# First two batches of a fused attention and mixing kernel: a scaled Abs in the weight conversion, softmax sums on VectorE, second-batch keys from transposed sums, and a searched order

## The chip, the cores and the metric

The kernel runs on one core of one Trainium2 chip. The metric is the device time of one execution in microseconds, taken as the median of three runs. A profiled execution of the same program gives the trace from which all rows below are taken.

## The reference, cut to what matters

Eight batches of 576 tokens go through three layers. The first is attention over 8 heads of 64 columns, with keys and values averaged over groups of 8 tokens (72 groups). The second turns the result by an angle and mixes tokens with two 576 by 576 matrices; the third is another pair of mixers, which the change does not touch.

```python
k_p = k.reshape(B, H, Sp, pool, D).mean(axis=3)          # pool = 8, Sp = 72
scores = scale * np.matmul(q, k_p.transpose(0, 1, 3, 2))
attn = np.exp(scores - np.max(scores, axis=-1, keepdims=True))
attn = attn / (np.sum(attn, axis=-1, keepdims=True) + 1e-09)
x = np.matmul(attn, v_p)                                  # then (B, 576, 512)
...
theta = x @ w_theta
yr = np.einsum('ts,bsd->btd', w_tok_r, x * np.cos(theta))
yi = np.einsum('ts,bsd->btd', w_tok_i, x * np.sin(theta))
u = x + yr + yi
u = u + np.maximum(u @ w_ch, 0.0)
```

The weights arrive as 64-bit floats and are converted to 32 bits on the chip.

## The kernel before, in words

The function `first_batches` holds batch 0 and the first part of batch 1, together with the conversion of `w_theta` and the nine 128-row slices of the two token mixers. It does not issue instructions directly. It hands each piece of work to a `Plan` as an operation with its engine, its estimated length and what it depends on; `Plan.run` then walks through time with a list scheduler and issues the operations in the order it finds. Later batches are written out by hand-set due times. At the very end a second scheduler, `Arrange`, takes the whole recorded program and fixes each engine's final order. So a change to the estimates or to the work of `first_batches` moves instructions on all engines.

The steps of batch 0, with the names that appear in the rows:

- **Keys.** `k` is loaded transposed (head columns on partitions), VectorE sums groups of 8 tokens into `sums`, and small copies put the scaled sums into `bdk`. For batch 1 the kernel before loads `k` with tokens on partitions (`nat_k`) instead, and TensorE sums the groups with a small matrix `pool`: per head pair four matmuls of 16 columns and two of 8 (line 420, `x<-pool,nat_k`).
- **Softmax.** TensorE forms scores (`x<-bdk,q`), VectorE takes the extreme per row (`mx`), ScalarE evaluates exponentials in 20 instructions of 72 columns per head pair, of which each also accumulates its sum (`e,ss<-x,mx`, line 2100). VectorE or GpSimd then scales `e` by the reciprocal `sm`.
- **Attend and angle.** `e` is transposed (`tp`, line 434), multiplied with the pooled values (`pt,vb`), giving `R`; five groups of four-pass 32-bit matmuls with `wt`, the converted `w_theta`, give the angle; sines follow, and `Z` (with a high and a low part) is x times cosine and sine.
- **Conversion.** 26 pieces: 8 of `w_theta`, 256 columns wide, and 18 of the token mixers, 288 columns wide. ScalarE takes the absolute value of the upper word, VectorE raises it to a floor (`most`, line 1951), shifts it by three bits and masks (line 1962), puts in the sign (line 1967) and the low bits (line 1972). For a mixer piece ScalarE then writes a rounded high part (`wtk`, line 1992) and GpSimd the remainder (line 1995).
- **Mixing.** 8 groups of 27 matmuls per batch, `m<-wtk,Z`. The first four take the first half of `Z`; groups of 256 columns need the first nine mixer pieces, groups of 320 columns need all 18. Each group goes through high times high, then the low part of `wtk`, then the low part of `Z`.

TensorE is kept busy while it has nothing else by `keep_busy`: matmuls of 512 columns on a constant tile (line 430, `m<-busy`), whose number the plan sets from its own estimate of the gap.

Of the kernel before, what the change touches and what calls it, by code (L numbers as in the profile page):

```python
# [57 lines left out]
F64_FLOOR = 2.0 ** -15  # L58
TH = ((0, 256), (256, 320))
TG = (2, 0, 1)  # L60
GUARD = range(26)
NK = 4
WARM = 800.0
LOWS = ()
WS = (0, 1)
ZL = (1, 1, 1)
EDVE = (2, 3)
NEAR = 20.0
# [3 lines left out]
class Arrange:  # L72
# [43 lines left out]
    def price(self, i):  # L116
# [27 lines left out]
        if e == "Activation":  # L144
            f = str(getattr(self.ins[i], "func", ""))
            table = "exp" if "Exp" in f else "sin" if "Sin" in f else None
            if op == "TensorCopy":
                return n * 0.833 + (52.0 if ps else 100.0), False, None
            return n * 0.833 + (62.0 if ps else 112.0) + (75.0 if len(ins) > 1 else 0.0), False, table
# [176 lines left out]
def tile_attn_moe(  # L326
# [1364 lines left out]
    class Plan:  # L1691

        LAT = {"PE": 170.0, "DVE": 110.0, "ACT": 120.0, "POOL": 110.0, "SP": 0.0}

        def __init__(self):
            self.ops = []
            self.users = {}
            self.dma = 3400.0  # L1700

        def add(self, ways, deps=(), homes=(), take=None, give=()):
            if isinstance(ways, tuple):
                ways = [ways]
            o = dict(ways=ways, deps=list(deps), take=take, give=give)
            for h in homes:
                o["deps"] += h.prior
                h.users.append(o)
            self.ops.append(o)
# [5 lines left out]
        def run(self, idle):  # L1715
            table = None
            for o in self.ops:
                o["rank"] = 0.0
            for o in reversed(self.ops):
                e, ns = o["ways"][0][0:2]  # L1720
                o["rank"] += (ns if e != "SP" else 2000.0) + self.LAT[e]
                for d in o["deps"]:
                    d["rank"] = max(d["rank"], o["rank"])
            free = {e: 0.0 for e in self.LAT}
            lock = 0.0
            todo = list(self.ops)
            while todo:
                best = []
                sp = False
                for o in todo:  # L1730
                    if any("end" not in d for d in o["deps"]):
                        continue
                    ready = max([0.0] + [d["end"] for d in o["deps"]])
                    if o["take"] is not None:
                        if not o["take"].free:
                            continue
                        ready = max(ready, o["take"].free[0][0])
                    for w in o["ways"]:
                        if w[0] == "SP":
                            if sp:  # L1740
                                continue
                            sp = True
                        s = max(ready, free[w[0]], lock + (90.0 if w[0] == "POOL" else 0.0) if w[2] is True else 0.0)
                        d = w[1]
                        if w[2] in ("exp", "sin") and w[2] != table:
                            d += 1290.0
                        best.append((s, s + d, o, w))
                s0 = min(b[0] for b in best)
                near = [b for b in best if b[0] <= s0 + NEAR]
                top = max(b[2]["rank"] for b in near)  # L1750
                o = [b[2] for b in near if b[2]["rank"] == top][0]
                s, end, o, w = min((b for b in best if b[2] is o), key=lambda b: b[1])
                todo.remove(o)
                e = w[0]
                if e == "PE":
                    idle(s, s - free["PE"])
                free[e] = end
                if w[2] is True:
                    lock = end
                elif w[2] is not False and e == "ACT":  # L1760
                    table = w[2]
                o["end"] = end + self.LAT[e]
                if e == "SP" and w[2]:
                    self.dma = max(self.dma, s + 3000.0) + w[2] * 1000.0 / 370.0
                    o["end"] = self.dma
                if o["take"] is not None:
                    o["take"].last = o["take"].free.pop(0)[1]
                w[3]()
                for g in o["give"]:
                    g.done(o["end"])  # L1770
# [15 lines left out]
    class Slots:  # L1786
        def __init__(self, names):
            self.free = [(0.0, n) for n in names]
            self.last = None

    class Held:


        def __init__(self, pool, readers):
            self.pool, self.n, self.t = pool, readers, 0.0
# [4 lines left out]

        def done(self, t):
            self.n -= 1
            self.t = max(self.t, t)
            if self.n == 0:
                self.pool.free.append((self.t, self.tag))
                self.pool.free.sort()

    def first_batches():
# [16 lines left out]
        EXP = 200.0  # L1825
# [4 lines left out]
        def ac(n):  # L1830
            return n * 0.86 + 65.0

        def po(n):
            return n * 2.1 + 147.0
# [25 lines left out]
        kn = {}  # L1860
# [31 lines left out]
        def fetch_k_pair(b, p):  # L1892
            h = kn[b]
            ds = slice(p * 128, (p + 1) * 128)
            k_at[b, p] = fetch(lambda: h()[:, 0:4, ds],
                               k01[b, 0:512, ds].rearrange("(c p) d -> p c d", p=128), 256, [h])

# [16 lines left out]
        kt_at = {}  # L1914
        for p in range(4):
            if p < NK:
                fetch_k_summed(0, p)
            elif p == NK:
                kn[0] = home("R0", [128, 5, 512], F32, "nat_k0")
                kt_at = {0: fetch_tail(kn[0], k01[0])}  # L1920
            if p >= NK:
                fetch_k_pair(0, p)
# [10 lines left out]
        def add_piece(i):  # L1933
# [10 lines left out]
            def absf():  # L1944
# [8 lines left out]
            def relu():  # L1953
                nc.scalar.activation(out=m_(), in_=m_(), func=ACTF.Relu, bias=floor[:, 0:1])

            def back():
                nc.gpsimd.tensor_scalar(
                    out=m_(), in0=m_(), scalar1=1.0, scalar2=F64_FLOOR, op0=ALU.mult, op1=ALU.add)

            def shl():  # L1960
                mu = m_().bitcast(U32)
                nc.vector.tensor_scalar(out=mu, in0=mu, scalar1=3, scalar2=0x3FFFFFFF,
                                        op0=ALU.logical_shift_left, op1=ALU.bitwise_and)

            def sign():
                mu = m_().bitcast(U32)
                nc.vector.scalar_tensor_tensor(out=mu, in0=box["t"][:, :, 1], scalar=0xC0000000, in1=mu,
# [7 lines left out]
            o = add(("ACT", ac(n), False, absf), [at], hs, take=mids)  # L1975
            if i in GUARD:
                o = add(("DVE", n * 0.521 + 65, True, most), [o], hs)
            else:
                o = add(("ACT", ac(n) + 60, False, relu), [o], hs)
                o = add(("POOL", n * 1.0 + 90, True, back), [o], hs)  # L1980
# [3 lines left out]
            if kind == "th":  # L1984
                conv[what[:3]] = add(("ACT", ac(n), False, lambda: nc.scalar.activation(
# [11 lines left out]
            x = add(("ACT", ac(n), False, hi), [o], hs + [w], give=[hold])  # L1997
# [13 lines left out]
        left = {}  # L2011

# [734 lines left out]
```

## Time and profile before

| | |
|---|---|
| median of three runs | 1255.43 us (1254.73 to 1256.89) |
| the profiled execution | 1259.36 us, span 1257.6 us |
| mean granted TensorE clock | 0.991 |
| TensorE busy | 1243.9 us (99%) |
| VectorE busy | 958.0 us (76%) |
| ScalarE busy | 672.1 us (53%) |
| GpSimd busy | 298.9 us (24%) |

The span runs from the first to the last instruction. Busy time of TensorE counts a matmul at a lowered clock, or one on the constant tile, like any other, so 99% does not say that all of it was needed work.

### The profile page before, as it was taken

How to read it: one execution, taken by the hardware profiler on the slowest of the kernel's cores; microseconds unless marked ns; L12 is line 12 of the kernel's file. 1: busy time of each engine (PE TensorE's matmuls, PEld its weight loads, DVE VectorE, ACT ScalarE, POOL GpSimd, SP SyncE). 2: the span in 40 equal slices, each digit the busy share in tenths (PEclk: the TensorE clock that was granted, in tenths of full speed). 3: DMA queues.
4: the chain of work that ended last, by engine and by line, in shares of the span. 5: the costliest groups of instructions: out<-in, count | busy, mean ns of one | idle time of the engine just before them, and what ended most of it. 6: DMA issues, size and time to landing. Idle time of an engine off the chain costs nothing.

```text
span 1257.6 us, 22368 instructions
## 1 busy us (share of the span) xinstructions
PE 1243.9 (99%) x8121; PEld 1207.9 (96%) x8123; DVE 958.0 (76%) x1723; ACT 672.1 (53%) x1405; POOL 298.9 (24%) x306
## 2 busy tenths in 40 slices
PE   8999999999999999999999999999999999999998
PEld 5889999999999999999999999999999999999998
DVE  6978868586767797867875679888644598988894
ACT  7887566666657564334322256666554544443442
POOL 1254423233241532211110011221000032123212
PEclk9979999999999999999999999999999999999999
DMA  9524323232321123657782487977448966546621
GB/s 339 162 70 136 126 93 97 68 114 70 109 71 54 38 84 125 233 195 250 251 296 76 158 273 250 299 250 249 160 138 306 342 225 220 173 141 220 207 84 69
DMA packets 122127, 214.51 MB, mean 171 GB/s; under 512 B 11744, under 2 KB 68576, under 8 KB 122016
## 3 DMA queue, kind: packets, MB, share of 16 engines
q1 hardware_dynamic: 122016, 213.08, 50.9%
q8 instruction: 64, 1.05, 0.3%
q14 instruction: 47, 0.39, 0.1%
HBM read 134.39 MB, written 78.64 MB: 169 GB/s over the span
## 4 chain that ended last, share of the span: by engine, by line
PE 92%; DVE 3%; DMA 2%; ACT 2%; issue 1%; POOL 0%; SPq 0%; DVEq 0%; ACTq 0%; POOLq 0%
PE m L420 33%; PE x L420 31%; PE t L420 23%; PE x L434 3%; ACT e L2100 1%; DMA scr_x<-u 1%; DMA ws<-w_ch 1%; DMA raw_e<-scr_g 0%; PE m L430 0%; PE t L434 0%; DVE raw_n L1416 0%; DVE u L1211 0%; PE m L434 0%; DMA scr_g<-p 0%; DVE ope_Xh L1413 0%
## 5 line engine op out<-in xcount | busy, mean ns | idle before, releaser
L420 PE MATMUL m<-wtk,Z 128*128 128x256 f32 (+1 forms) x1536 | 255.9, 302 | 1.3 <-ACT wtk L1992 1.3
L420 PEld LDWEIGHTS m<-wtk,Z 128*128 128x128 f32 x1536 | 222.7, 191 | 4.2 <-ACT wtk L1992 3.0
L420 PE MATMUL x<-ope_Z,wa 128*128 128x384 f32 x492 | 94.8, 336 | 0.0
L420 PEld LDWEIGHTS x<-ope_Z,wa 128*128 128x128 f32 x492 | 86.4, 188 | 0.0
L1665 POOL TENSOR_TENSOR o<-o,u 128x384 f32<-128x384 f32 x12 | 16.4, 1386 | 268.4 <-DMA raw_Z<-scr_g 167.1
L1034 POOL TENSOR_TENSOR Z<-tmp,Z 128x1024 fp32r<-128x1024 f32 x26 | 63.2, 2442 | 69.5 <-ACT Z L1033 69.5
L1314 POOL TENSOR_TENSOR wo<-wm,wo 128x256 fp32r<-128x256 f32 (+2 forms) x36 | 31.1, 867 | 180.3 <-ACT wo L1313 174.0
L420 PE MATMUL t<-wth,Xh 128*128 128x256 f32 x448 | 62.2, 279 | 0.0
L420 PE MATMUL m<-wtk,zt 128*128 128x256 f32 (+1 forms) x192 | 57.8, 302 | 0.3 <-ACT wtk L1992 0.3
L420 PEld LDWEIGHTS t<-wth,Xh 128*128 128x128 f32 x448 | 57.5, 188 | 0.5
L420 PE MATMUL m<-ope_Z,wa 128*128 128x384 f32 x234 | 48.2, 336 | 0.0
L420 PE MATMUL t<-ope_Z,wa 128*128 128x384 f32 x234 | 48.0, 335 | 0.0
L1019 DVE TENSOR_TENSOR tmp<-x,tmp 128x1024 f32<-128x1024 f32 x26 | 31.7, 1220 | 18.0 <-PE x L434 15.3
L420 PE MATMUL x<-ope_R,wa 128*128 128x384 f32 x228 | 43.8, 337 | 0.0
L420 PE MATMUL x<-bdk,q 128*128 128x144 f32 x298 | 43.2, 296 | 0.4 <-ACT bdk L2014 0.4
L420 PE MATMUL t<-ope_Xl,wa 128*128 128x384 f32 x204 | 42.4, 336 | 0.0
L420 PE MATMUL m<-ope_Xl,wa 128*128 128x384 f32 x204 | 42.3, 336 | 0.0
L420 PEld LDWEIGHTS x<-bdk,q 128*128 128x128 f32 x298 | 40.3, 198 | 1.5 <-ACT bdk L2014 1.1
L420 PEld LDWEIGHTS m<-ope_Z,wa 128*128 128x128 f32 x234 | 41.5, 188 | 0.0
L420 PEld LDWEIGHTS t<-ope_Z,wa 128*128 128x128 f32 x234 | 41.4, 188 | 0.0
L1299 POOL TENSOR_TENSOR wsum<-wm 128x128 f32<-128x128 f32 (+1 forms) x18 | 12.4, 690 | 119.4 <-DVE wm L1289 118.6
L1574 DVE TENSOR_TENSOR p<-p,u 128x384 f32<-128x384 f32 x36 | 20.5, 568 | 26.5 <-ACT p L1573 26.5
(480 smaller groups left out, 3544.0 us busy)
## 6 DMA issues: line engine op xcount, KB each, us to landing
wa<-scr_w SPq DMA_DIRECT2D x42, 512.0 KB, 5.4
scr_g<-g SPq DMA_DIRECT2D x108, 192.0 KB, 3.0
scr_w<-wo SPq DMA_DIRECT2D x42, 256.0 KB, 3.4
scr_u<-R SPq DMA_DIRECT2D x32, 288.0 KB, 2.1
u<-scr_u SPq DMA_DIRECT2D x32, 288.0 KB, 4.2
scr_w<-wo SPq DMA_DIRECT2D x18, 512.0 KB, 5.7
scr_x<-u SPq DMA_DIRECT2D x32, 288.0 KB, 2.2
raw_n<-scr_x SPq DMA_DIRECT2D x24, 384.0 KB, 4.1
```

Of the source, the lines that this page charges most:

```text
L420: nc.tensor.matmul(out=o, lhsT=l, rhs=r, start=start, stop=stop, skip_group_check=skip)
L434: nc.tensor.transpose(o, i, ident)
L1019: nc.vector.tensor_tensor(out=tmp, in0=px.unsqueeze(1).to_broadcast([128, 2, 512]), in1=tmp, op=ALU.mult)
L1034: later(1.0 if lo is nc.vector else 0.0, lambda: lo.tensor_sub(out=zl, in0=zv, in1=zh.bitcast(F32)), tg, zg)
L1299: nc.gpsimd.tensor_tensor(out=s[:, 2], in0=a11, in1=a21, op=ALU.subtract)
L1314: eng.tensor_sub(out=o[:, :, 1], in0=src, in1=o[:, :, 0].bitcast(F32))
L1574: nc.vector.tensor_add(out=p5[ih].t, in0=p5[ih].t, in1=u2[ih].t)
L1665: nc.gpsimd.tensor_tensor(out=u22[d].t, in0=u22[d].t, in1=u2[d].t, op=ALU.add)
L2100: nc.scalar.activation(out=e()[:, c, 2 * p + h, :], in_=box["v"][:, c - c0, h], func=ACTF.Exp, scale=-1.0, bias=mx[i][:, c, h:h + 1], accu ...
```

## The change

Six things are edited, all within the first two batches:

1. The absolute value in the conversion carries a scale of 2 to the -112, and the floor instruction `most` goes (26 of them). The shift loses its mask, and the sign mask changes from two bits to one.
2. The 80 exponentials of the first two batches no longer accumulate; per head pair one VectorE reduction over 720 columns forms the sums.
3. The keys of batch 1 are loaded transposed and summed on VectorE, as batch 2 already did; the 24 matmuls with `pool` and their copies go.
4. Nine of the 18 low parts of `wtk`, and the four low parts of the split `w_theta`, move from GpSimd to VectorE.
5. The plan's estimates of latencies and lengths change, and a search of 400 seeded variations of the priorities picks the order with the lowest estimated end.
6. `Arrange` counts 92 ns more for a ScalarE instruction with two outputs.

The core of the diff:

```diff
+TRIES = 400
+SEED = 2
+LOWS = range(0, 26, 2)
+WS = (1, 2)
+SOFTMAX = "BBBBBBBB"
...
-                nc.scalar.activation(out=m_(), in_=box["t"][:, :, 1].bitcast(F32), func=ACTF.Abs)
-
-            def most():
-                nc.vector.tensor_scalar(out=m_(), in0=m_(), scalar1=F64_FLOOR, scalar2=None, op0=ALU.max)
+                nc.scalar.activation(out=m_(), in_=box["t"][:, :, 1].bitcast(F32), func=ACTF.Abs, scale=F64_SCALE)
...
-                nc.vector.tensor_scalar(out=mu, in0=mu, scalar1=3, scalar2=0x3FFFFFFF,
-                                        op0=ALU.logical_shift_left, op1=ALU.bitwise_and)
+                nc.vector.tensor_scalar(out=mu, in0=mu, scalar1=3, scalar2=None, op0=ALU.logical_shift_left)
...
         def keys(b, p):
-            if (b, p) in ks_h:
+            if b == 0:
                 return keys_summed(b, p)
...
-                for c in range(4):
-                    mm(o[:, 8 + 16 * c:24 + 16 * c], kh()[:, c, ds], pm()[:, 0:16], True, True)
-                for c0 in (0, 72):
-                    mm(o[:, c0:c0 + 8], kh()[0:64, 4, ds], pm()[0:64, 0:8], True, True)
...
+            if p % 2 == 0:
+                pair_at[b] = next_keys(b, p // 2)
+            return pair_at[b]
...
-                                bias=mx[i][:, c, h:h + 1], accum_out=ss[i][:, c, h:h + 1])
+                                bias=mx[i][:, c, h:h + 1], **acc)
...
+            if mode != "C":
+                es = [add(("DVE", dv(720), False, lambda: nc.vector.tensor_reduce(
+                    out=ss[i], in_=ep(), axis=AX.X, op=ALU.add)), es + last.get(("ss", i), []), [e])]
...
+            for _ in range(tries):
+                p = list(prio)
+                k = draw.randrange(n)
+                v = draw.choice((-30e3, -10e3, -4e3, -1.5e3, 1.5e3, 4e3, 10e3, 30e3))
+                for i in range(k, min(n, k + draw.choice((1, 1, 2, 4, 8, 16)))):
+                    p[i] += v
+                c, o = self.trial(p)
+                if c <= cost:
+                    prio, cost, out = p, c, o
```

The order moves in three places that matter below. First TensorE, at the end of the angle's matmuls of batch 0 (`wt,R`; `con,R` are transposes of the result). Before, the last of them are followed by the key sums of batch 1 and the first mixing matmuls:

```order
L434 MATMUL t_651<-con,R_423 128x128 x4
L434 MATMUL x_658<-con,R_423 128x128 x4
L420 MATMUL t_666<-pool,nat_k_386 128x16 x4
L420 MATMUL t_666<-pool,nat_k_386 128x8 x2
L420 MATMUL m_782<-wtk_502,Z_584 128x256
L420 MATMUL m_782<-wtk_505,Z_584 128x256
```

In the changed program the same place reads:

```order
L423 MATMUL x_569<-wt_386,R_407 128x256 x8
L423 MATMUL x_602<-wt_386,R_407 128x256
L423 MATMUL m_592<-wtk_538,Z_558 128x256
L423 MATMUL m_592<-wtk_481,Z_558 128x256
L423 MATMUL m_592<-wtk_483,Z_558 128x256
L423 MATMUL m_592<-wtk_567,Z_558 128x256
```

The matmuls with `pool` are gone, and the first mixing group (`m_592`) starts inside the last angle group.

Second VectorE, at the end of the softmax of batch 0. Before:

```order
L2114 TENSOR_SCALAR sm_106<-ss_104 128x10
L2117 RECIPROCAL sm_106<-sm_106 128x10
L2121 TENSOR_TENSOR e<-e,sm_106 128x5x144
L1844 COPY pt_341<-x_326 128x320
L2114 TENSOR_SCALAR sm_107<-ss_105 128x10
L2117 RECIPROCAL sm_107<-sm_107 128x10
L2121 TENSOR_TENSOR e<-e,sm_107 128x5x144
```

Changed, two sums over 720 columns stand ahead of the two scalings:

```order
L2170 TENSOR_REDUCE ss_104<-e 128x5x2
L2172 TENSOR_SCALAR sm_106<-ss_104 128x10
L2175 RECIPROCAL sm_106<-sm_106 128x10
L2170 TENSOR_REDUCE ss_105<-e 128x5x2
L2179 TENSOR_TENSOR e<-e,sm_106 128x5x144
L2172 TENSOR_SCALAR sm_107<-ss_105 128x10
L2175 RECIPROCAL sm_107<-sm_107 128x10
L2179 TENSOR_TENSOR e<-e,sm_107 128x5x144
```

Third TensorE again, where in the changed program the first group of 320 columns (`m_760`) begins. It is the first that needs the second halves of `wtk`, and it comes right behind the pooled values of batch 1:

```order
L423 MATMUL x_734<-nat_v_645,pool 128x512 x4
L423 MATMUL m_760<-wtk_538,Z_558 128x320
L423 MATMUL m_760<-wtk_481,Z_558 128x320
L423 MATMUL m_760<-wtk_483,Z_558 128x320
L423 MATMUL m_760<-wtk_567,Z_558 128x320
L423 MATMUL m_760<-wtk_560,Z_558 128x320
L423 MATMUL m_760<-wtk_496,Z_558 128x320
L423 MATMUL t_773<-bdk,q_271 128x144 x3
L423 MATMUL m_760<-wtk_625,Z_558 128x320
L423 MATMUL m_760<-wtk_578,Z_558 128x320
L423 MATMUL m_760<-wtk_447,zt_616 128x320
```

Before, the first such group is likewise behind the two groups of 256 columns, but batch 1's scores stand ahead of it there, and here only one part of them does (`t_773`).

## Rows read from the trace of the kernel before

**Rows 1.** The page: busy time by engine, and the granted clock in 40 slices.

```profile
PE 1243.9 (99%) x8121; PEld 1207.9 (96%) x8123; DVE 958.0 (76%) x1723; ACT 672.1 (53%) x1405; POOL 298.9 (24%) x306
...
PEclk9979999999999999999999999999999999999999
```

**Rows 2.** Windows: stretch, length, busy per engine, granted clock, DMA share and rate.

```profile
22.00:50.00 28.00, 27.67 (x123) 20.57 (x123) 27.08 (x74) 24.36 (x60) 5.59 (x7) 1.00 0.85 270
58.28:71.94 13.66, 13.66 (x61) 13.54 (x60) 7.33 (x25) 9.16 (x45) 0.06 (x1) 0.50 0.15 44
85.59:92.42 6.83, 6.53 (x24) 5.85 (x24) 5.44 (x15) 6.80 (x32) 6.42 (x9) 0.50 0.23 73
55.00:110.00 55.00, 52.69 (x301) 47.54 (x302) 44.47 (x97) 44.93 (x162) 30.74 (x29) 0.81 0.29 90
```

**Rows 3.** Timeline of TensorE up to 54 us: start, length, instructions, idle before.

```profile
9.91 1.03 PE L430 MATMUL m<-busy 128*128 128x512 bf16 x4
...
12.02 2.75 PE L430 MATMUL m<-busy 128*128 128x512 bf16 x11
...
25.50 0.77 PE L420 MATMUL x<-pt,vb 128*128 128x320 f32 x2
26.60 0.78 PE L420 MATMUL x<-t,vl 128*128 128x320 f32 x2 [0.33 <-DVE vl L2190]
...
30.02 0.60 PE L434 MATMUL x<-con,e 128*128 128x128 f32 x4
...
34.34 7.07 PE L420 MATMUL x<-wt,R 128*128 128x256 f32 x32
...
53.77 1.50 PE L420 MATMUL t<-pool,nat_k 128*128 128x16 f32 x12
```

**Rows 4.** Windows of the instructions on `nat_k` alone: their four stretches summed.

```profile
sum 8.18, PE 8.17 PEld 7.95; mean PE 2.04 PEld 1.99
```

**Rows 5.** Timeline of ScalarE: the first exponentials and the last.

```profile
8.61 0.32 ACT L2100 ACTIVATE e<-x,mx 128x72 f32<-128x72 f32 x1 [3.91 <-DVE mx L2095]
8.82 0.19 ACT L2100 ACTIVATION_READ_ACCUMULATOR e<-x,mx 128x1 f32 x1
8.92 0.31 ACT L2100 ACTIVATE e<-x,mx 128x72 f32<-128x72 f32 x1
...
21.48 0.44 ACT L2100 ACTIVATE e<-x,mx 128x72 f32<-128x72 f32 x1
```

**Rows 6.** Timeline of VectorE: the last scaling, and three conversions side by side.

```profile
22.56 0.91 DVE L2121 TENSOR_TENSOR e<-e,sm 128x720 f32<-128x720 f32 x1
...
36.40 0.74 DVE L1962 TENSOR_SCALAR early<-early 128x288 uint32<-128x288 uint32 x3
37.06 1.18 DVE L1967 SCALAR_TENSOR_TENSOR early<-early,early 128x288 uint32<-128x288 uint32 x3
38.16 1.18 DVE L1972 SCALAR_TENSOR_TENSOR early<-early,early 128x288 uint32<-128x288 uint32 x3
```

**Rows 7.** Timeline of TensorE, 74 to 85 us: mixing, and a wait for `wtk`.

```profile
77.52 1.10 PE L420 MATMUL m<-wtk,Z 128*128 128x256 f32 x8
...
84.35 0.41 PE L420 MATMUL m<-wtk,Z 128*128 128x320 f32 x1 [1.29 <-ACT wtk L1992]
```

**Rows 8.** Groups of VectorE up to 100 us: busy us, mean ns, idle before.

```profile
L1972 DVE SCALAR_TENSOR_TENSOR early<-early,early 128x288 uint32<-128x288 uint32 (+1 forms) x18 | 10.3, 599 | 0.0
...
L1972 DVE SCALAR_TENSOR_TENSOR early<-early_w,early 128x288 uint32<-128x288 uint32 x4 | 1.7, 446 | 0.0
```

**Rows 9.** Timelines of GpSimd and of VectorE at 39 us, side by side.

```profile
39.15 2.73 POOL L1995 TENSOR_TENSOR wtk<-early,wtk 128x288 fp32r<-128x288 f32 x3 [4.48 <-DMA early<-w_tok]
46.52 2.32 POOL L1995 TENSOR_TENSOR wtk<-early,wtk 128x288 fp32r<-128x288 f32 x3 [4.63 <-ACT wtk L1992]
...
40.09 1.14 DVE L1951 TENSOR_SCALAR early<-early 128x288 f32<-128x288 f32 x2
41.14 1.35 DVE L1962 TENSOR_SCALAR early<-early 128x288 uint32<-128x288 uint32 x3
```

More of the change, by code (lines that the diff above doesn't have):

```diff
@@ L2 @@
 import math
+import random
 from contextlib import ExitStack
@@ L1704, in add @@
                 ways = [ways]
-            o = dict(ways=ways, deps=list(deps), take=take, give=give)
+            o = dict(ways=ways, deps=list(deps), take=take, give=give, hold=take and take.pending)
             for h in homes:
@@ L1713, in home, with prepare @@
             return Home(self, tag, shape, dt, name)
-        def run(self, idle):
-            table = None
+        def prepare(self):
+            n = len(self.ops)
+            self.after = [[] for _ in range(n)]
+            self.first = [0] * n
             for o in self.ops:
-                o["rank"] = 0.0
-            for o in reversed(self.ops):
[L1720 to L1737, printed above, removed]
-                    for w in o["ways"]:
-                        if w[0] == "SP":
-                            if sp:
-                                continue
-                            sp = True
-                        s = max(ready, free[w[0]], lock + (90.0 if w[0] == "POOL" else 0.0) if w[2] is True else 0.0)
-                        d = w[1]
-                        if w[2] in ("exp", "sin") and w[2] != table:
[L1746 to L1765, printed above, removed]
-                if o["take"] is not None:
-                    o["take"].last = o["take"].free.pop(0)[1]
@@ new lines, in prepare @@
+                o["deps"] = sorted({d["i"] for d in o["deps"]})
+                self.first[o["i"]] = len(o["deps"])
+                for d in o["deps"]:
+                    self.after[d].append(o["i"])
+            self.rank = [0.0] * n
+            for o in reversed(self.ops):
+                i = o["i"]
+                e, ns, kb = o["ways"][0][0:3]
+                own = 430.0 + kb * 1024.0 / 262.0 + 1750.0 if e == "SP" else ns + self.TAIL[e]
+                self.rank[i] = own + max([0.0] + [self.rank[k] + self.LAT[self.ops[k]["ways"][0][0]] for k in self.after[i]])
@@ new lines, in run @@
+        def run(self, idle, tries):
+            self.prepare()
+            draw = random.Random(SEED)
+            prio = list(self.rank)
+            cost, out = self.trial(prio)
+            n = len(prio)
+            for _ in range(tries):
[7 more added lines that the diff above has]
+                    prio, cost, out = p, c, o
+            free = 0.0
+            for s, i, w, slot in sorted(out, key=lambda x: x[0]):
+                o = self.ops[i]
+                if w[0] == "PE":
+                    idle(s, s - free)
+                    free = s + w[1]
+                if slot is not None:
+                    o["take"].last = slot
@@ L1768, in run @@
                 w[3]()
-                for g in o["give"]:
-                    g.done(o["end"])
     class Home:
@@ L1787, in __init__ @@
         def __init__(self, names):
-            self.free = [(0.0, n) for n in names]
-            self.last = None
+            self.names = list(names)
+            self.pending = self.last = None
     class Held:
         def __init__(self, pool, readers):
-            self.pool, self.n, self.t = pool, readers, 0.0
+            self.pool, self.n = pool, readers
+            pool.pending = self
         def name(self):
@@ L1973, in low3 @@
                                                op0=ALU.logical_shift_right, op1=ALU.bitwise_or)
[L1975 to L1980, printed above, removed]
+            o = add(("ACT", acs(n), False, absf), [at], hs, take=mids)
             o = add(("DVE", n * 0.521 + 65, True, shl), [o], hs)
@@ L2559, in first_batches @@
                 next_keys(2, g)
-        pl.run(idle)
+        pl.run(idle, TRIES)
         cq_done[0] = 100
```

195 lines of the change are left out of this document (134 added, 61 removed).

## The prediction

> **What bounds the kernel now.** I read the page first, then windows over the first 110 us, then TensorE's timeline there. The page says that TensorE is busy for 99% of the span [rows 1], so a change pays only where TensorE does work that is not needed, works at the lower clock, or is idle. All of this lies early: the row of granted clocks is below 9 only in the third slice [rows 1], which the windows resolve into two stretches at 0.50, that is 1.2 GHz, from 58.28 to 71.94 and from 85.59 to 92.42 us [rows 2]. Between 55 and 110 us TensorE is also idle for 55.00 - 52.69 = 2.3 us [rows 2]. Ahead of that, up to the attend matmuls at 25.50, it mostly fills time on the constant tile while the softmax of batch 0 runs on ScalarE and VectorE [rows 3]. From 22 to 50 us VectorE is busy for 27.08 of 28.00 us [rows 2]: it is the engine that comes next.
>
> So everything is to be won before 110 us, and whatever TensorE gets through earlier there comes off the end, since behind it TensorE is full.
>
> **The change part by part.**
>
> *Key sums of batch 1.* The matmuls with `pool` take 8.2 us of TensorE altogether [rows 4]; they go. In their place VectorE sums two tiles of 1152 columns. The price per column is that of three conversions of 288 columns in 1.10 us [rows 6], 0.37 each, which I read as 1.04 ns a column plus 0.07: 1.27 us per tile. The first lies within the VectorE sum below, the second behind it; half as many copies remain on ScalarE. Gain 8.2.
>
> *The clock.* The first stretch at half clock begins 4.5 us after the first of the key sums, at 53.77 [rows 3], and TensorE is without a gap from there (13.66 of 13.66 us busy, [rows 2]); what is new in its work are matmuls of 8 and 16 columns. In the changed order mixing matmuls of 256 columns stand in that place. I take it that this fall goes. Of its 13.66 us some 5.2 are themselves key sums (half of the four stretches are at half clock and nearly twice as long: 2.6 + 2.6 of the 8.2), and the other 8.4 shrink to half: gain 4.2. Bounds: 0 if the clock falls all the same, 4.2 if not. The second stretch, 6.83 us, is worth 3.4; the row just ahead of it is a wait of 1.29 us for `wtk`, which ended at 84.35 [rows 7]. The idle 2.3 us between 55 and 110 are gained as well; what takes their place is charged below.
>
> *Exponentials without sums.* With its sum, one takes 8.92 - 8.61 = 0.31 us, of which the accumulator read is 0.10 [rows 5]. Without it I take 0.21 (bounds 0.15, as there is less to wait for, and 0.31, if the pitch is not the read's doing). Before, they end at 21.48 + 0.29 = 21.8 [rows 5]. The changed order puts 18 fillers between the scores of the second and third head pair; at the place of the 4 that started at 9.91 and at some 0.22 us each (11 in 2.75, with the last one's drain, [rows 3]) they hold the third pair to 13.9. Its transfers are no later: the load of the values, moved ahead of two of them, is covered by these same fillers, and without them it would cost about a us. Scores of three chunks and their reduction take some 1.5 us (estimate: 0.75 and 0.5 at the pitches above, and the handover), so the last 20 exponentials run from 15.4 to 19.6. Then come, in order, one sum of 720 columns (0.82), the scaling of the third pair (0.83), the two small instructions (0.2) and the scaling of the last: 22.4, where before it ended at 22.56 + 0.91 = 23.5 [rows 6]. From there to the attend matmuls I keep before's 2.0: 24.4 instead of 25.50. The attend stretch before lasts 34.34 - 25.50 = 8.84, with a wait of 0.33 and transposes of 0.43 [rows 3], both of which the changed order has ahead of it: 8.1. The angle's matmuls start at 32.5 instead of 34.34. Gain 1.9; bounds 0 and 4.2 (20 + 20 exponentials at 0.10 less, were nothing else late).
>
> *The conversion, and what is late next.* The floor instruction goes: 26 times 0.22, the pitch of the shift next to it [rows 6], 5.7 us off VectorE. Added there are the low parts: 9 of 288 columns (0.37) and 4 of 512 (0.60), 5.7 in all, and the sums. VectorE thus keeps its load, and the question is when the last mixer pieces are done, because the first group of 320 columns needs all 18. From 22.4 the changed order has on VectorE up to the last of them: 8 pieces of `w_theta` at 0.87, 18 mixer pieces at 0.96 (0.22 + 0.37 + 0.37, [rows 6]), and 26 other instructions with 12,576 columns together (copies, mask, roundings, products, low parts, one split, one key sum): 7.0 + 17.2 + 14.9 = 39.1 us. GpSimd still does 7 low parts in that time. When three of them ran from 39.15 to 41.88, five VectorE instructions that take 1.1 took 2.3 [rows 9]: 0.4 lost per low part, 2.8 in all. With ScalarE's last rounding (0.33) the last `wtk` is there at 64.7.
>
> TensorE comes there at: 32.5, plus 19.4 for the five angle groups with their transposes (34.34 to 53.77, [rows 3]), plus two groups of 27 mixing matmuls at 0.12 (8 in 1.10 with the drain, [rows 7]), 6.6, plus 3.5 for the pooled values (8 passes of 512 columns, at 0.22 per 256 as in the angle's row, [rows 3]), plus 1.3 for the six matmuls and three scores ahead: 63.3. It waits 1.4 us, and some 0.6 for the low parts after that: **2.0**. Bounds: 0, if VectorE loses nothing to GpSimd, and 6. A wait of 1.29 us stood ahead of the second fall of the clock [rows 7]; I let the clock fall here once for 6.83 us as it did there [rows 2]: **3.4** (bounds 0 and 6.8).
>
> The Trainium skill's page "SBUF — State Buffer" (section "SBUF: two separate sides") says that VectorE and GpSimd take their shared port pair as an exclusive lock for a whole instruction, and that the loser blocks fully. By that rule each low part would cost VectorE its full 0.77 us (three in 2.32, [rows 9]), 5.4 in all, and the wait would be 4.0, not 1.4. The rows show something between: in groups the low-bits instruction took 599 ns on the mean where GpSimd was active and 446 elsewhere [rows 8].
>
> *Batch 1 behind it.* Its scores, exponentials, sums and scalings now come after the 18 pieces, while TensorE has half of the mixing left, four groups or some 14 us, to cover them. Two sums of 0.82 are new in that chain, and the last attend matmuls are followed at once by the angle's, which need their copies (0.33 and 0.4): **2.0**, bounds 0.5 and 4. GpSimd's scalings are unchanged.
>
> *The rest.* The conversion's scale and the simpler masks change no count beside those above. The extra 92 ns in `Arrange` only steer the order of what had two outputs.
>
> **The sum.** 8.2 + 4.2 + 3.4 + 2.3 + 1.9 = 20.0 gained; 2.0 + 3.4 + 2.0 = 7.4 given back; 12.6 net. It is made on the profiled execution of 1259.36 us, 3.9 over the median of the runs; in it I expect 1246.8, and as a median 1255.43 - 12.6 = **1242.8 us**.
>
> **The rivals**, with chances.
> - *As forecast* (0.45): 1240 to 1246.
> - *The lock blocks fully* (0.10): 2.6 us more waiting on VectorE, 1245.4. For it: the stretched rows; against: [rows 8] show a mean loss of a third. This is the page's rule.
> - *The clock never falls* (0.20): nothing at half clock after the start, and the chain of batch 1 hidden but for 1 us: 20.0 - 2.0 - 1.0 = 17.0, 1238.4, or down to 1235 if VectorE is early too. For it: TensorE has mixing work in all places of the front but one.
> - *The clock falls twice, or for as long as the first time before* (0.17): a second fall of 13.66 us costs 6.8 more, 1249.6; one long fall in place of the short one costs 3.4 more, 1246.2. For it: transposes with waits between them stand ahead of the attend matmuls, and TensorE is idle there.
> - *The key sums were not the cause, and nothing else improves* (0.03): within 0.2% of before. 0.2% (2.5 us) is about what a measurement can tell from no change.
> - *Slower* (0.05): VectorE is the bound. If it ends the conversions at 71 instead of 64.7 (ScalarE's and VectorE's fixed orders blocking each other), TensorE waits 6 us more, runs the next 13.66 us at half clock (6.8), and the 12.6 are gone; it decides from there on. Against it: VectorE waited hardly at all between 22 and 50 us before, with the same load [rows 2].
>
> Range 1236 to 1250: it leaves out the early end of the third case, the late end of the fourth, and the last two, some 0.19. Faster by over 0.2%: 0.91; within: 0.04; slower: 0.05.
>
> **What would show it.** Exponentials at a pitch near 0.21 and ending near 19.6; attend matmuls near 24.4; the angle near 32.5; no key sums on TensorE, and the full clock from 53 to 63 us; one wait of TensorE for `wtk` of 1 to 4 us at 63, with a stretch at 0.50 behind it; the first angle group of batch 1 some 12 us earlier than before. The prediction is wrong if the clock falls in the middle of gapless mixing, or if TensorE waits elsewhere for more than 3 us.

## The result, and the profile after

The changed kernel takes 1242.82 us (median of four executions, 1242.40 to 1242.96), against 1256.16 for the kernel before (1254.73 to 1258.72): a ratio of 0.9891 [0.9874, 0.9908]. Its profiled execution took 1242.70 us; that of before had taken 1259.36. Of the 16.7 us by which the profiled span is shorter (1257.6 to 1240.9), 14.3 are busy time of TensorE (1243.9 to 1229.6), the rest its idle time.

The page of the changed kernel, busy time by engine and the granted clock, beside [rows 1]:

```profile
PE 1229.6 (99%) x8076; PEld 1193.8 (96%) x8076; DVE 961.4 (77%) x1717; ACT 666.2 (54%) x1324; POOL 285.8 (23%) x293
...
PEclk9999999999999999999999999999999999999999
```

No slice is at the lower clock. The window that was at 0.81 before [rows 2] now reads:

```profile
55.00:110.00 55.00, 53.42 (x379) 49.22 (x378) 50.85 (x105) 43.95 (x123) 20.98 (x19) 1.00 0.36 109
```

In the same 55 us the trace has 379 matmuls of TensorE, not 301, although it is idle for almost as long (1.6 us against 2.3). TensorE's timeline, to be held against [rows 3, 7]: the start of attend, of the angle, of the mixing, and the wait for the second halves of `wtk`.

```profile
24.55 0.81 PE L423 MATMUL t<-pt,vb 128*128 128x320 f32 x2 [0.37 <-DVE t L1931]
...
32.47 10.50 PE L423 MATMUL x<-wt,R 128*128 128x256 f32 x40
...
48.36 0.97 PE L423 MATMUL m<-wtk,Z 128*128 128x256 f32 x6 [0.19 <-ACT Z L2507]
...
65.54 0.78 PE L423 MATMUL m<-wtk,Z 128*128 128x320 f32 x2 [1.45 <-ACT wtk L2049]
```

ScalarE's exponentials, beside [rows 5]: the first group, the first of the third head pair, and the last.

```profile
8.13 2.01 ACT L2149 ACTIVATE e<-x,mx 128x72 f32<-128x72 f32 x9 [0.94 <-DVE mx L2138]
...
14.90 0.95 ACT L2149 ACTIVATE e<-t,mx 128x72 f32<-128x72 f32 x4 [2.19 <-DVE mx L2138]
...
17.63 2.05 ACT L2149 ACTIVATE e<-x,mx 128x72 f32<-128x72 f32 x9
```

Their pitch is 0.20 us, they end at 19.68, and 2.19 us of idle time are left in the middle. The last cast of a `wtk` (a rounded high part) on ScalarE, first in the changed kernel, then in the kernel before:

```profile
65.80 0.43 ACT L2049 CAST wtk<-early 128x288 fp32r<-128x288 f32 x1
```

```profile
86.29 0.43 ACT L1992 CAST wtk<-early 128x288 fp32r<-128x288 f32 x1
```

It ends at 66.2 us, where it ended at 86.7: a move of 20.5 us, more than the whole gain, and the experiments turn on it. I call it the *end of the conversions*.

### The profile page after: what moved, and what is told of

It is laid out like the page before. It is cut to its first block, busy times and chain, and to the rows that moved or that the text cites. A ratio compares the mean times of both kernels' runs of the same rounds, so it can differ in the third digit from the quotient of the medians.

```text
span 1240.9 us, 22149 instructions
## 1 busy us (share of the span) xinstructions
PE 1229.6 (99%) x8076; PEld 1193.8 (96%) x8076; DVE 961.4 (77%) x1717; ACT 666.2 (54%) x1324; POOL 285.8 (23%) x293
## 4 chain that ended last, share of the span: by engine, by line
PE 91%; DMA 4%; DVE 2%; ACT 1%; issue 1%; SPq 1%; ACTq 0%; DVEq 0%
PE m L423 33%; PE x L423 31%; PE t L423 23%; PE x L437 3%; DMA early<-w_tok 1%; DMA pool<-pool 1%; DMA ws<-w_ch 1%; DMA raw_e<-scr_g 0%; DMA early<-w_theta 0%; PE t L437 0%; SPq L1927 0%; DVE early L2034 0%; PE m L437 0%; DMA scr_u<-R 0%; DVE early L2029 0%
## 5 line engine op out<-in xcount | busy, mean ns | idle before, releaser
L423 PE MATMUL m<-wtk,Z 128*128 128x320 f32 (+1 forms) x1536 | 253.4, 300 | 1.6 <-ACT wtk L2049 1.4
L423 PEld LDWEIGHTS m<-wtk,Z 128*128 128x128 f32 x1536 | 218.5, 188 | 3.9 <-ACT wtk L2049 2.1
L423 PEld LDWEIGHTS x<-ope_R,wa 128*128 128x128 f32 x228 | 39.9, 188 | 0.6 <-DVE p L1581 0.6
L423 PE MATMUL x<-opo_Z,wa 128*128 128x384 f32 x216 | 40.4, 336 | 0.0
L1577 DVE TENSOR_TENSOR p<-p,u 128x384 f32<-128x384 f32 x36 | 20.5, 569 | 25.4 <-ACT p L1576 25.4
```

Source lines behind the costliest of these rows:

```text
L423: nc.tensor.matmul(out=o, lhsT=l, rhs=r, start=start, stop=stop, skip_group_check=skip)
L1577: nc.vector.tensor_add(out=p5[ih].t, in0=p5[ih].t, in1=u2[ih].t)
```

## The experiments

Two theories. **The prediction's**: the gain is TensorE's own work and clock (key sums 8.2, falls of the clock 7.6, the first of which the key sums cause), with VectorE just about keeping up. **The rival**: VectorE's conversions are the bound; the key sums only filled a wait for them, and what counts is when the conversions end. The twelve runs came in three groups, each on one chip beside the kernel before, whose medians there were 1256.47, 1258.81 and 1256.40 us. Between groups I compare ratios; the changed kernel has 0.9891, and in the third group 0.9887 [0.9863, 0.9910]. Differences in us across groups are those of the medians, which for the kernel before differ by up to 2.7 us from group to group.

**e1. The key sums alone, in the kernel before.**

```diff
+            if b == 1:
+                if p % 2 == 0:
+                    pair_at[b] = next_keys(b, p // 2)
+                return pair_at[b]
...
-            fetch_k_pair(1, p)
```

> The kernel before, with one part of the change alone: the keys of batch 1 come from transposed sums on VectorE, the matmuls with pool are gone; floor, accumulated sums, the old scheduler and its estimates stay. If the key sums cost 8.2 us and also bring the first fall of the clock (the prediction's step), the gain is 8.2 + 4.2 = 12.4 less up to 1 for VectorE: about 1244, and the granted clock is full from 53 to 66 us. Rival: the first fall has another cause and stays, then only 5.7 to 8.2 are gained, 1248 to 1250, and a slice near 60 us still shows a lower clock.

Measured: 1258.67 us, ratio 1.0015 [1.0002, 1.0028]. Nothing is gained. Windows of this kernel (length, then busy time of TensorE, of its weight loads, VectorE, ScalarE, GpSimd, the clock), and three rows of TensorE:

```profile
70.00:75.00 5.00, 3.17 (x9) 1.90 (x8) 5.00 (x14) 4.99 (x11) 3.12 (x4) 0.50 0.01 2
75.00:80.00 5.00, 0.93 (x4) 0.79 (x4) 5.00 (x5) 4.45 (x13) 5.00 (x5) 0.50 0.00 0
80.00:85.00 5.00, 4.13 (x15) 3.41 (x14) 5.00 (x10) 3.60 (x21) 4.31 (x6) 0.50 0.00 0
```

```profile
68.98 1.62 PE L420 MATMUL x<-bdk,q 128*128 128x144 f32 x6 [1.51 <-ACT e L2106]
...
74.50 0.64 PE L420 MATMUL m<-wtk,Z 128*128 128x320 f32 x1 [1.35 <-ACT wtk L1992]
...
79.21 1.33 PE L420 MATMUL x<-bdk,q 128*128 128x144 f32 x4 [4.07 <-ACT e L2106]
```

VectorE, which now does the key sums as well, is busy for all 15 of these 15 us, TensorE for 8.2. The conversions end at 81.83 + 0.43 = 82.3, and TensorE waits for them and for batch 1's exponentials. The work that was taken out had covered these waits. The longest, 4.07 us, is for exponentials that ScalarE began at 77.84, although VectorE had their `mx` ready at 72.34 + 0.45 = 72.8: casts and a table load stood ahead of them. ScalarE's timeline:

```profile
74.36 2.17 ACT L2472 CAST wth<-wt 128x512 fp32r<-128x512 f32 x4
76.55 1.28 ACT L2106 ACT_TABLE_LOAD   x1
77.84 0.32 ACT L2106 ACTIVATE e<-x,mx 128x72 f32<-128x72 f32 x1
```

So ScalarE's order has a part in these waits, beside VectorE's conversions.

In the kernel before, it was VectorE that waited at this place: between 40 and 73 us 6.3 us in all for TensorE's scores and key sums, which from 58.28 on ran at half clock. Of these, 4.6 us (groups of VectorE: count, busy, mean ns, idle):

```profile
L2095 DVE TENSOR_REDUCE mx<-x 128x4 f32<-128x288 f32 x2 | 0.9, 458 | 3.1 <-PE x L420 3.1
...
L2017 DVE TENSOR_SCALAR bdk<-x 64x72 f32<-64x72 f32 x2 | 0.5, 230 | 1.5 <-PE x L420 1.5
```

In e1 VectorE does not wait for TensorE there, and still the conversions end only 4.4 us earlier.

The sign that I had set for the clock did come: it is full from 53 to 66 us, and the fall of before at 58.28 is gone. But a stretch of 17.1 us at 0.50 begins at 69.20, right behind the wait of 1.51 us, and all ten executions have a mean clock of 0.990 to 0.993. So this fall comes with no narrow key sum left in the program. The time fits neither predicted outcome (1244, or 1248 to 1250). The rival theory fits in that the key sums had filled waits; that VectorE alone is the bound is not shown by this run.

**e2. 24 narrow matmuls more, in the changed kernel**, in front of the first two mixing groups.

```diff
+                                for r in range(2):
+                                    zs = z_t[0, 0][:, 0, jj, 2 * r, 0:128].bitcast(F32)
+                                    for c in range(4):
+                                        mm(box["o"][:, 16 * c:16 * c + 16], zs, con[:, 0:16], True, True)
+                                    for c in range(2):
+                                        mm(box["o"][:, 8 * c:8 * c + 8], zs[0:64], con[0:64, 0:8], True, True)
```

> The changed kernel with 24 matmuls of 8 and 16 columns more, put in front of the first two mixing groups (12 at about 48 us, 12 some 4 us later), in place of the key sums' matmuls of before but with no load, copy or VectorE work of their own; their results are overwritten. At the full clock they are 48 records of 0.125 us, 6.0 us, of which up to 2 may be hidden in the waits near 65 us. If narrow matmuls make the clock fall (the prediction's step), 6.8 us come on top: 1253.6 to 1255.6, and a stretch of 13.66 us at 0.50 that begins some 4 us after the first of them. Rival: the clock stays full, 1246.8 to 1248.8.

Measured: 1249.64 us, ratio 0.9946 [0.9927, 0.9965], 6.8 us more than the changed kernel. The two halves in TensorE's timeline, 12 matmuls with 24 records each, and a window behind the first:

```profile
48.35 3.03 PE L423 MATMUL m<-con,Z 128*128 128x16 f32 x24
...
60.63 3.03 PE L423 MATMUL m<-con,Z 128*128 128x16 f32 x24
```

```profile
52.46:55.86 3.40, 3.40 (x10) 2.69 (x10) 3.28 (x7) 3.30 (x7) 0.94 (x1) 0.55 0.00 0
```

The clock does fall behind the first half, though TensorE was never idle there, but for 3.4 us, a quarter of what I expected; behind the second half it does not fall. So the price lies between the two expectations: 6.0 for the matmuls, and the fall's 1.7 less what is saved because TensorE does not wait for `wtk` any more. The conversions end at 72.4 here, 6.2 us later than in the changed kernel, with less than a full load on VectorE: it waits 3.9 us for the second mixing group on TensorE. So the end of the conversions is itself held by TensorE when TensorE is late.

**e3. The changed kernel with the keys of batch 1 back on TensorE.**

```diff
-            if p % 2 == 0:
-                pair_at[b] = next_keys(b, p // 2)
-            return pair_at[b]
...
+            a = add(("PE", 1340.0, False, go), [k_at[b, p], kt_at[b], pm_at[0]], [kh, pm], take=banks)
...
+            return [add([("ACT", ac(72), False, cp(h, scaled_act)), ("DVE", dv(72), False, cp(h, scaled_dve))],
```

> The changed kernel with the keys of batch 1 back on TensorE (24 matmuls with pool on nat_k, copies by either engine); the search runs on the changed plan and finds another order. If the prediction's two terms hold here too, 8.2 + 4.2 are lost again: about 1255, with a fall of the clock near the key sums. Rival: only the matmuls at the full clock cost, 5.7: about 1248.5, with the clock full.

Measured: 1247.81 us (1245.47 to 1249.70), ratio 0.9938 [0.9918, 0.9958]: 5.0 more by the medians and 5.9 by the ratios, as the rival had it. The profiled execution, the fastest of the five, has the full clock throughout; of the others one has a mean clock of 0.998. Two of the four lots, from TensorE's timeline:

```profile
59.98 1.50 PE L423 MATMUL x<-pool,nat_k 128*128 128x16 f32 x12
...
64.89 1.50 PE L423 MATMUL t<-pool,nat_k 128*128 128x16 f32 x12
```

There is no wait for `wtk` in this kernel: the conversions end at 63.7, 2.5 us earlier, as VectorE is spared the two sums, and the second lot stands where the changed kernel waits at 65.54. With the same matmuls as before and no fall in this execution, the key sums alone are not enough to bring one.

**e4. The order alone**: the new plan, estimates and search, with the old work. Beside the edit of e3 and a floor as in e6, here known to the plan:

```diff
-LOWS = range(0, 26, 2)
-WS = (1, 2)
+LOWS = ()
+WS = (0, 1)
...
-SOFTMAX = "BBBBBBBB"
+SOFTMAX = "CCCCCCCC"
```

> The new plan, estimates and search alone: floor instruction (as a maximum with 0), accumulated exponentials, keys by pool and all low parts on GpSimd as before. By the prediction's terms the order itself was given no price but the waits, so most of the gain goes: 8.2 + 4.2 + 1.9 lost, about 1255 (within 0.2% of before). Rival: the searched order is worth 5 us or more by itself (fewer waits, shorter stretch at half clock): 1250 or less.

Measured: 1259.82 us, ratio 1.0024 [1.0005, 1.0044]. The order alone gains nothing. Two windows, the angle's first row, and key sums:

```profile
60.00:65.00 5.00, 5.00 (x24) 4.94 (x23) 3.98 (x15) 1.92 (x13) 0.00 (x0) 0.50 0.00 0
...
75.00:80.00 5.00, 1.98 (x7) 1.75 (x8) 5.00 (x10) 4.97 (x19) 3.22 (x4) 0.67 0.01 4
```

```profile
32.70 3.62 PE L423 MATMUL t<-wt,R 128*128 128x256 f32 x16
...
54.55 2.43 PE L423 MATMUL x<-pool,nat_k 64*128 64x8 f32 x16
```

Again TensorE is idle for 3 of 5 us (75 to 80) while VectorE is full; the conversions end at 80.4. The angle, however, starts at 32.70, with accumulating exponentials. The first fall, 10.2 us from 56.25, begins among key sums (the last row), with TensorE busy without a gap, as in the kernel before.

**e5. The work alone**: all edits of the work in the kernel before, with its old scheduler. Beside the edit of e1:

```diff
-LOWS = ()
-WS = (0, 1)
+LOWS = range(0, 26, 2)
+WS = (1, 2)
...
-                o = add(("DVE", n * 0.521 + 65, True, most), [o], hs)
...
-                                bias=mx[i][:, c, h:h + 1], accum_out=ss[i][:, c, h:h + 1])
+                                bias=mx[i][:, c, h:h + 1])
...
+            es = [add(("DVE", dv(720), False, lambda: nc.vector.tensor_reduce(
+                out=ss[i], in_=ep(), axis=AX.X, op=ALU.add)), es + last.get(("ss", i), []), [e])]
```

> The kernel before with all the edits of the work (scaled absolute value and no floor, sums on VectorE, keys of batch 1 from transposed sums, 13 low parts on VectorE), and with the old scheduler and its old estimates: the opposite half of the run that changed the order alone. If the work carries the gain by itself, as the prediction priced it, 1242 to 1246. Rival: the work pays only in an order that fits it, because TensorE then waits for the conversions as it did when the key sums alone were taken out: 1250 or more, with waits for wtk and exponentials between 60 and 85 us.

Measured: 1248.91 us, ratio 0.9912 [0.9888, 0.9936], conversions ending at 72.3 and 6.8 us at half clock; the angle starts at 32.88. The work alone brings most of the gain; with the order it is 0.9891, but the two intervals overlap, so the order's share on top of it is not settled by this pair.

**e6. The floor back, in the changed kernel** (as a maximum with 0, unknown to the plan).

```diff
             def shl():
+                nc.vector.tensor_scalar(out=m_(), in0=m_(), scalar1=0.0, scalar2=None, op0=ALU.max)
                 mu = m_().bitcast(U32)
```

> The changed kernel with an instruction of the floor's form back on VectorE (a maximum with 0, 26 times 0.22 us, which changes no value); the plan does not know of it. If VectorE's conversions set the wait at 65 us (the prediction's next bound), all 5.7 us show there: 1247 to 1249, and 1250 to 1252 if the clock falls behind the longer wait. Rival: VectorE has slack and the wait is ScalarE's: 1245 or less.

Measured: 1250.85 us, ratio 0.9928 [0.9909, 0.9948]. The waits in TensorE's timeline:

```profile
65.63 1.08 PE L423 MATMUL t<-bdk,q 128*128 128x144 f32 x6 [2.95 <-ACT bdk L2073]
...
71.15 1.00 PE L423 MATMUL m<-wtk,Z 128*128 128x320 f32 x2 [2.65 <-ACT wtk L2050]
```

The conversions end at 71.41 + 0.43 = 71.8, that is 5.6 later, for 5.7 us more on VectorE. The clock is at half for 10.2 us behind the first wait. In the changed kernel VectorE is the bound at this place without any slack.

**e7. The 13 low parts back on GpSimd.**

```diff
-                ways = [("DVE", dv(n), True, low(nc.vector))]
+                ways = [("DVE", dv(n), True, low(nc.gpsimd))]
...
-            split_w.extend([x, add([("POOL", po(512), True, low(nc.gpsimd)), ("DVE", dv(512), True, low(nc.vector))][WS[0]:WS[1]],
+            split_w.extend([x, add([("POOL", po(512), True, low(nc.gpsimd)), ("DVE", dv(512), True, low(nc.gpsimd))][WS[0]:WS[1]],
```

> The changed kernel with the 13 low parts that moved to VectorE back on GpSimd. VectorE is freed of 5.7 us. At 0.4 us lost per low part of 288 columns, and some 0.7 per one of 512 (the rows of before), it loses 6.4: no change to 1244. By the rule of a full lock (the rival), it loses their whole time, 9 of 0.77 and 4 of some 1.3, 12.1, net 6.4 more: about 1249.

Measured: 1251.54 us, ratio 0.9938 [0.9917, 0.9959]. TensorE's longest wait in the timeline, and then VectorE's shift and GpSimd's low parts in groups from 30 to 73 us (count, busy, mean ns, idle):

```profile
71.78 1.00 PE L423 MATMUL m<-wtk,Z 128*128 128x320 f32 x2 [5.37 <-ACT wtk L2049]
```

```profile
L2025 DVE TENSOR_SCALAR early<-early 128x288 uint32<-128x288 uint32 x16 | 9.6, 610 | 0.0
```

```profile
L2052 POOL TENSOR_TENSOR wtk<-early,wtk 128x288 fp32r<-128x288 f32 x15 | 15.0, 1014 | 18.0 <-ACT wtk L2049 18.0
```

The same shift in the changed kernel, from 30 to 73 us:

```profile
L2025 DVE TENSOR_SCALAR early<-early 128x288 uint32<-128x288 uint32 x16 | 5.6, 362 | 0.0
```

VectorE was freed of 5.7 us, yet the conversions end at 72.03 + 0.44 = 72.5, 6.2 later: the low parts on GpSimd held VectorE up by some 12 us, near the 12.1 of a full lock and not my 6.4. Of this, 1.8 are a wait of VectorE for ScalarE ahead of a rounding, which the changed kernel does not have, so the lock's own share is some 10 of 12.1.

**e8. Accumulating exponentials in the changed kernel, without the eight sums.**

```diff
-                            acc = dict(accum_out=ss[i][:, c, h:h + 1]) if mode == "C" else {}
+                            acc = dict(accum_out=ss[i][:, c, h:h + 1])
...
-                    out=ss[i], in_=ep(), axis=AX.X, op=ALU.add)), es + last.get(("ss", i), []), [e])]
+                es = [add(("DVE", dv(720), False, lambda: None), es + last.get(("ss", i), []), [e])]
```

> The changed kernel with accumulating exponentials, and without the eight sums of 720 columns on VectorE. By the prediction's step the angle's matmuls start 1.9 us later, near 34.4, and the time is about 1244.7. Rival: VectorE, freed of 0.9 us per head pair, ends its conversions earlier and gives this back at the wait for wtk: 1242.8 or less.

Measured: 1247.26 us, ratio 0.9899 [0.9877, 0.9921], not distinguishable from the changed kernel. Two rows of TensorE:

```profile
32.67 1.67 PE L423 MATMUL x<-wt,R 128*128 128x256 f32 x7
...
66.86 0.78 PE L423 MATMUL m<-wtk,Z 128*128 128x320 f32 x2 [2.79 <-ACT wtk L2049]
```

The angle starts 0.2 us later, not 1.9: the exponentials end at 21.5, 1.8 later, but the last scaling is spared two sums of 0.90 us ahead of it. A shift of 0.2 us tells little: in the two profiles of the changed kernel itself the angle starts at 32.47 and at 32.34. The conversions end at 67.5, 1.3 later, although VectorE has less to do; why is not settled.

**e9 to e12**, on one chip. First the changed kernel once more:

> The changed kernel once more, beside the three that follow, as their measure: 1242.4 to 1243.0, the clock full. If the chip matters as much for it as it seemed to for the kernel before, up to 1246.

Measured: 1242.61 us (1241.74 to 1244.56). In its profiled execution (1243.10 us) the clock fell behind the same wait of 1.44 us for `wtk`, which in the first profile had no effect:

```profile
65.00:70.00 5.00, 4.56 (x20) 4.20 (x21) 5.00 (x9) 4.39 (x9) 1.84 (x2) 0.73 0.29 108
```

The stretch is 3.4 us long. One program thus runs with and without a fall behind the same wait.

**e10. The load of the values behind the queries of batch 0** (its rank in `Arrange` set just under theirs).

```diff
+        sp = [i for i, e in enumerate(self.eng) if e == "SP" and self.acc[i][0]]
+        q = [i for i in sp if self.acc[i][0][0]["name"].startswith(("q0", "q1"))][:4]
+        v = [i for i in sp if self.acc[i][0][0]["name"].startswith("nat_v")][0]
+        r[v] = min(r[i] for i in q) - 1.0
```

> The changed kernel with the load of batch 0's values issued behind the queries of the third and fourth head pair, not ahead of them; nothing else is edited. In the changed kernel's profile the third pair's queries landed at 12.9 us and ScalarE was idle for 2.19 us ahead of its exponentials. If that landing holds the softmax, the idle time goes, the exponentials end at 17.5 to 18.5 in place of 19.7, and 1 to 2 us are gained: 1241 to 1242. Rival (the prediction's step): the transfers are covered by the fillers, which hold the third pair in any case, and the values now come late for their pooling near 16 us: 1242.8 or more.

Measured: 1241.99 us (1241.19 to 1243.30), ratio 0.9881 [0.9858, 0.9904], against 1242.61 beside it. The last exponentials on ScalarE, and TensorE's rows:

```profile
15.68 1.91 ACT L2153 ACTIVATE e<-x,mx 128x72 f32<-128x72 f32 x8
```

```profile
30.50 10.50 PE L427 MATMUL x<-wt,R 128*128 128x256 f32 x40
...
64.45 0.78 PE L427 MATMUL m<-wtk,Z 128*128 128x320 f32 x2 [0.80 <-ACT wtk L2053]
```

The exponentials end at 17.6 and the angle starts 2.0 us earlier than in the changed kernel. The transfers were not covered, as I had said they were. But the conversions end only 1.1 earlier, and 0.6 us remain in the medians, less than the intervals can tell. It is the fastest median of all, and no proven improvement.

**e11. No search.**

```diff
-TRIES = 400
+TRIES = 0
```

> The changed kernel with the plan's first order, without the 400 variations of the search; estimates and work unchanged. If the search is worth what the order was in the other runs (5 to 6 us with the new work), 1246 to 1249, with a longer wait for wtk near 65 us. Rival: the new estimates do it alone, 1244 or less.

Measured: 1249.54 us, ratio 0.9940 [0.9917, 0.9963], 6.9 us more than the changed kernel beside it. But in the profile (1248.72 us) there is no long wait for `wtk` near 65 (0.32 and 0.56 us) and the clock is full: the angle starts at 33.62, and later there is, among others, this wait for VectorE's work on `e`:

```profile
121.75 0.63 PE L437 MATMUL x<-con,R 128*128 128x128 f32 x4 [1.86 <-DVE e L804]
```

The size was as expected, the place was not: beside e9, the angle starts 1.3 us later and TensorE is idle for 3.5 us between 110 and 160, where e9 has no idle time.

**e12. The wait of e7 filled** with 44 matmuls of 256 columns. Beside the edit of e7:

```diff
+                            if half == 0 and jj == 0 and t0 == 256:
+                                for r in range(44):
+                                    mm(box["o"][:, 0:256], z_t[0, 0][:, 0, 0, r % 4, 0:128],
+                                       wtk[r % 9][:, 0, 0:256], True, True)
```

> The kernel with the 13 low parts on GpSimd, in which TensorE waited 2.4 and 5.4 us near 65 to 72 and the clock was at half from 70 to 77 (1251.5), with 44 matmuls of 256 columns, 5.2 us, put at the head of the first group of 320 columns; their results are overwritten. They fill most of the wait. If the idle time brings the fall of the clock, the fall goes and the time drops by about 3 although there is more work: 1248 to 1249. Rival: the fall has another cause, then nothing is gained: 1251 or more.

Measured: 1251.76 us, ratio 0.9961 [0.9946, 0.9975].

```profile
72.29 1.00 PE L423 MATMUL m<-wtk,Z 128*128 128x320 f32 x2 [3.40 <-ACT wtk L2049]
```

```profile
70.00:75.00 5.00, 2.71 (x10) 2.55 (x11) 4.96 (x12) 2.74 (x6) 2.72 (x4) 0.61 0.00 0
```

The matmuls went into the wait, of which 3.4 us remained, and the clock fell in it all the same, for 6.8 us as in e7. Since the wait was not closed, this does not tell whether idle time is the cause.

## Why the prediction was right, and where its steps were not

The median came out as predicted, 1242.8 us, but several terms were wrong and cancelled, so the agreement to 0.1 us is luck. (The gain was to be 12.6 and is 13.3; a fourth execution had moved the median of before from 1255.43 to 1256.16.) That the gain is TensorE's own work and clock fits the profiles: 14.3 of the 16.7 us are busy time. What the prediction did not see is that taking the key sums out brings nothing by itself.

- **Key sums, 8.2.** As matmuls at the full clock they are 6.0 (e2), and putting them back costs 5.0 (e3). Replaced alone they are worth nothing (e1). What failed is the reading that they were needless work on the path: without them, in the order before, TensorE waits for VectorE, which is full from 65 to 85 us, and for ScalarE (e1). They pay together with the other edits, by which the conversions end at 66 instead of 87 us (e1 against e3). My sum held for all edits together since it priced VectorE's chain in the changed order: 64.7 predicted for the last `wtk`, 66.2 measured.
- **The first fall of the clock, 4.2, put down to the key sums.** At its place the step held, as a gain of its own it failed. The fall at 58.28 goes when they go (e1), and the three falls that come without a gap on TensorE (before, e4, e2) all stand among or behind narrow matmuls. But narrow matmuls need not bring one (e3, the second half of e2), and without them, in the order before, a longer one comes behind waits (e1). In e5 to e9 and e12 the fall stands at or behind a wait of TensorE; yet waits of 1.45 us in the changed kernel and of 1.86 us in e11 have none behind them. That narrow matmuls or waits are the cause is argued, not shown; e12 could not settle it.
- **The size of both falls, 7.6.** It was taken from one execution with 13.66 + 6.83 us at half clock [rows 2], but an execution of the kernel before can have hardly any. Of the 20 in the first group, the seven with a mean clock of 0.999 or more took 1252.68 to 1254.89 us, median 1254.4, so that the falls are worth some 2 us in the median of 1256.5, and some 5 in the profiled 1259.36 (an estimate across chips). The prediction carried a sum made on one long execution over to the median.
- **What made up for it.** I charged 3.4 for a fall that the changed kernel does not have in its first profile, and in e9 has for 3.4 us, 1.7 in time. I charged 2.0 for batch 1's chain; TensorE waits for 0.1 us between 70 and 125 us in the changed kernel. So 5.4 us of charges hardly came due, against falls overpriced by some 5.5 in the median. By its mechanism the first profile is my third rival (the clock never falls, batch 1 hidden): the two profiled executions differ by 16.7, near its 17.0, the medians by 13.3, near the forecast.
- **Batch 1's first angle group, 12 us earlier.** It starts at 97.34 instead of 105.14, 7.8 earlier. The sign was badly chosen: 195 matmuls of mixing stand ahead of it in the trace, where 128 stood before.
- **Exponentials and the angle's start, 1.9.** The value was right (19.68 for 19.6, 24.55 for 24.4, 32.47 for 32.5), the reason was not: with accumulation in the changed order the angle starts at 32.67 (e8) or 32.70 (e4), and with the new work in the old order at 32.88 (e5). Either brings most of it, and the two do not add up. And the third pair was held by its queries, not by fillers (e10).
- **The wait for the second half of `wtk`, 2.0.** 1.45 measured, at the place named. VectorE is the bound there: 5.7 us more on it end the conversions 5.6 later (e6).
- **The low parts on GpSimd, 0.4 each.** Mis-sized. By e7 they cost VectorE most of their length, some 10 to 12 us of 12.1. The Trainium skill's page "SBUF — State Buffer" (section "SBUF: two separate sides") states an exclusive lock for a whole instruction, and e7's figure is near it. In the changed kernel the conversions end 1.5 us later than I had summed, of the 2.6 that the rival with this rule added; TensorE came 0.8 later too, so that little of it shows in the wait.

## What to carry to other kernels

Before work on the fullest engine is priced as a gain, look for the wait that it covers: find what the next engine delivers, and when, if the work is gone. Take the cost of a falling clock from several executions, since one profile may hold an unusually long fall. When two edits each move the same start, as the order and the new work did here, one can undo each alone before giving either the credit.

## What the runs showed of the hardware

The stretches at half clock in these profiles, the program's last microseconds aside, were 3.4, 6.8, 10.2, 17.1 and 20.5 us in all, and a stretch in which TensorE waits costs less than half its length: in the 17.07 us of e1 TensorE is busy for 10.29, so that at most half of that, some 5.1 us, can be lost (an estimate).

```profile
69.20:86.27 17.07, 10.29 (x33) 7.86 (x32) 17.07 (x31) 15.09 (x53) 13.63 (x13) 0.50 0.07 25
```

A shift of 288 columns on VectorE takes 0.30 us alone and 0.90 beside a low part on GpSimd, and the low part itself grows from 0.80 to over 1.0 us; the changed kernel's timelines of the two engines:

```profile
61.60 0.90 DVE L2025 TENSOR_SCALAR early<-early 128x288 uint32<-128x288 uint32 x1
62.42 0.91 DVE L2025 TENSOR_SCALAR cvt<-cvt 128x288 uint32<-128x288 uint32 x1
63.26 0.29 DVE L2025 TENSOR_SCALAR early<-early 128x288 uint32<-128x288 uint32 x1
```

```profile
52.15 0.80 POOL L2052 TENSOR_TENSOR wtk<-early,wtk 128x288 fp32r<-128x288 f32 x1 [5.12 <-ACT wtk L2049]
59.77 3.40 POOL L2052 TENSOR_TENSOR wtk<-early,wtk 128x288 fp32r<-128x288 f32 x3 [6.82 <-ACT wtk L2049]
```
